# Preparing three heads at a time on 120 rows, with the first two inverses ordered on VectorE, in a chunked recurrence followed by an MLP

## The chip, the cores and the metric

The kernel runs on one core of a Trainium2 chip. The metric is the device time of one execution in microseconds (us); the median of several runs is compared. TensorE does the matmuls, VectorE and ScalarE the elementwise work and the copies out of PSUM, GpSimd (POOL) issues part of the DMAs, and SyncE (SP) issues the rest.

## The reference

For 4 batches and 8 heads a state of 40 x 40 is carried over 768 steps; its output goes through an MLP with the Mish function (`h * tanh(softplus(h))`):

```python
for t in range(S):
    y[:, :, t] = np.einsum('bhd,bhde->bhe', rt, state)
    Sa = np.einsum('bhde,bhe->bhd', state, at)
    state_decay = state * wt[:, :, None, :] - np.einsum('bhd,bhe->bhde', Sa, bt)
    state = state_decay + np.einsum('bhd,bhe->bhde', vt, kt)
...
h = x @ w_in                       # 3072 x 320 by 320 x 2048
sp = np.where(h > 20.0, h, np.log1p(np.exp(np.minimum(h, 20.0))))
g = h * np.tanh(sp)
return (g @ w_out).astype(np.float32)
```

## The kernel before, in words

The 768 steps are cut into 12 chunks of 64, and the chunks are worked in six pairs. Within a chunk the steps depend on each other through a triangular system, which is solved with an explicit inverse, so that all that is left to do in sequence is one pass for each chunk.

For each chunk there is a **preparation**, `pre_a`, called twice (`be` = 0, 1). A call holds two blocks of 40 rows (one for each dimension of a head), on partitions 0 to 39 and 64 to 103, with eight heads of the batches side by side: 80 of 128 partitions carry data. It loads `w` and `a` (L131, tile `wa`) and `b` and `k` (L134, tile `bk`) on SP's queue. VectorE forms the running products of `w` forward and backward with two scans (L147 and L157), after a small reduction (L145), reciprocals (L146, L156) and a copy (L150), and multiplies them into `a` (L152) and into `b` and `k` (L170). ScalarE copies `a` into the layout `ad` (L155). TensorE multiplies `ad` by `bk` (L186, 16 matmuls in the profile for each call, since a float32 matmul shows as two) and transposes `bk` (L202); four matmuls with the identity (L166) bring the chunk's decay factors into the tile `rw`. GpSimd writes the forward products to the DRAM scratch `pD`.

For each pair there is an **inverse**: `pre_inv` on VectorE alone, a transpose (L209), 30 elimination steps of two instructions each (L214 and L216, each step reading what the one before wrote), and two transposes (L218, L220). Then `post_inv` on TensorE and ScalarE (L232, L241, L258).

For each chunk there is a **step**, `step(c)`, which carries the state (L284, L293, L304, L314, L334 and L339 on TensorE; masks and state updates on VectorE, L316, L325, L342, L346). It writes its result to the DRAM scratch `yD`.

The **MLP** runs after the attention. Its float32 matmuls are done as sums of products of a high and a low part, so the weights are split first: w_in in 12 pieces and w_out in 8. The weights arrive as 64-bit floats: a piece is loaded as 512 KB (L453, tile `cv_d`), scaled on ScalarE (L459), put together in three VectorE instructions (L461 to L463), and split by ScalarE (L494) and VectorE (L495). Three of the w_in pieces (`early`, with `NQ0 = 1` quarter) are split at the beginning, beside the first pair; the other nine by `first`, when the last pair's preparation is over, with one buffer for each stage (`CVA = 1`). The w_out pieces follow. The x tiles are loaded from `yD` and `pD` and split on VectorE (L567, L569, L570). L585 is the first matmul of the MLP, L605 to L607 the second.

What sets the order: the program is written with a Tile scheduler that orders each engine's instructions by the order of the code and by priorities, the table `OFF` (a larger number moves an instruction's place further forward). Each engine then runs its list strictly in order. `ORDER = '0aiA1'` says what is written around a pair: step of the first chunk, preparation of a later pair (`a`), the next inverse (`i`), the weights (`A`), step of the second chunk. The letters of `QS` choose the queues of the loads (SP), and of the steps' loads, `yD` and `pD` (GpSimd).

## Time and profile before

| | us |
|---|---|
| median of 3 runs (lowest, highest) | 846.35 (843.54, 848.62) |
| the profiled execution | 842.54 |
| its span | 840.7 |
| beginning of inverse 0, end of inverse 0 | 48.7, 99.0 |
| beginning of inverse 5, end of inverse 5 | 383.5, 433.6 |
| first matmul of the MLP | 471.7 |

The profile is of one execution, and its times are counted from the start of its span. PE is TensorE's matmul, PEld its weight load, DVE is VectorE, ACT ScalarE, POOL GpSimd, SP SyncE. A row of a group names a line of the kernel, the engine, the operation, output<-input, how often it occurred, and then busy us, the mean of one in ns, and the idle time of the engine just before, with what ended it. PEclk is the share of the full clock that TensorE was granted. What bounds a stage is read from that stage's own window and from the waits in it, not from the mean over the span.

### The profile page before, as it was taken

Reading aid. Unit: us, or ns where it says so; the run is one execution under the profiler, and the core shown is the slowest. Engines: PE = TensorE matmul, PEld = TensorE weight load, DVE = VectorE, ACT = ScalarE, POOL = GpSimd, SP = SyncE. Lnnn points to the kernel's source line nnn. Section 1 sums busy time; section 2 is a strip of 40 time slices with the busy share of each in tenths; the row PEclk is TensorE's granted clock in tenths of the full one; section 3 lists DMA queues with packets and bytes.
Section 4 is the critical chain, followed back from the end, with each engine's and each line's share of the span. In section 5 each row is a group of like instructions: output and inputs, shape, how many; then the busy total and the mean of one; then the engine's idle time right before and its main releaser. Section 6 shows DMA issues by size and latency. Waiting matters only on the chain.

```text
span 840.7 us, 18817 instructions
## 1 busy us (share of the span) xinstructions
PE 737.5 (88%) x7816; PEld 688.5 (82%) x7816; DVE 463.3 (55%) x975; ACT 427.9 (51%) x937; POOL 103.3 (12%) x182
## 2 busy tenths in 40 slices
PE   2545898998989889888749999999999999999998
PEld 2444687887778778777648899999999999999998
DVE  6789889659879758947962649221222222122110
ACT  4533657774665766676457646333333333333331
POOL 8100021132123023211210200000000000000000
PEclk9755699899999999999978999999999999999999
DMA  6422232333333133313543744211120121100000
GB/s 173 139 72 64 82 78 67 96 75 94 89 96 88 57 86 98 96 26 98 139 123 82 186 132 127 54 39 32 38 54 29 26 54 36 35 20 16 16 1 32
DMA packets 58213, 61.92 MB, mean 74 GB/s; under 512 B 25536, under 2 KB 48704, under 8 KB 58128
## 3 DMA queue, kind: packets, MB, share of 16 engines
q1 hardware_dynamic: 49296, 40.94, 17.4%
q0 software_dynamic: 8832, 19.79, 9.4%
q8 instruction: 61, 1.00, 0.5%
q14 instruction: 24, 0.20, 0.1%
HBM read 48.79 MB, written 11.86 MB: 72 GB/s over the span
## 4 chain that ended last, share of the span: by engine, by line
PE 61%; ACT 15%; DVE 15%; DMA 5%; issue 4%; SPq 0%; POOL 0%; ACTq 0%; DVEq 0%
PE ph L585 20%; PE po L605 7%; PE po L606 7%; PE po L607 6%; PE pa L186 4%; PE pa L258 3%; PE pq L314 3%; PE pq L334 2%; DMA cv_d<-in_wi 2%; DVE XL L216 2%; DVE tmp L214 2%; ACT KT L260 2%; ACT bdT L250 1%; ACT bdT L249 1%; ACT ad L155 1%
## 5 line engine op out<-in xcount | busy, mean ns | idle before, releaser
L585 PE MATMUL ph<-xh,w_ih 128*128 128x256 f32 x576 | 148.9, 283 | 0.0
L587 ACT ACTIVATE g<-ph 128x512 f32<-128x512 f32 x96 | 57.3, 598 | 179.7 <-PE ph L585 179.7
L591 DVE TENSOR_TENSOR gl<-g,gh 128x1024 fp32r<-128x1024 f32 x48 | 58.6, 1224 | 160.3 <-ACT gh L590 160.0
L585 PE MATMUL ph<-xh,w_il 128*128 128x256 f32 x576 | 123.7, 283 | 0.0
L186 PE MATMUL pa<-bk,ad 128*128 128x168 f32 x384 | 85.5, 372 | 42.2 <-DVE bk L170 15.0
L606 PE MATMUL po<-w_ol,gh 128*128 128x320 f32 x384 | 118.6, 309 | 0.0
L607 PE MATMUL po<-w_oh,gl 128*128 128x320 f32 x384 | 118.3, 309 | 0.0
L605 PE MATMUL po<-w_oh,gh 128*128 128x320 f32 x384 | 117.8, 309 | 0.1
L585 PEld LDWEIGHTS ph<-xh,w_ih 128*128 128x128 f32 x576 | 109.5, 190 | 0.2 <-issue 0.2
L186 PEld LDWEIGHTS pa<-bk,ad 128*128 128x128 f32 x384 | 70.4, 232 | 47.6 <-issue 23.1
L585 PE MATMUL ph<-xl,w_ih 128*128 128x256 f32 x384 | 100.7, 284 | 0.0
L585 PEld LDWEIGHTS ph<-xh,w_il 128*128 128x128 f32 x576 | 96.2, 190 | 0.1
L585 PEld LDWEIGHTS ph<-xl,w_ih 128*128 128x128 f32 x384 | 73.1, 190 | 0.2 <-issue 0.2
L605 PEld LDWEIGHTS po<-w_oh,gh 128*128 128x128 f32 x384 | 71.8, 188 | 0.6 <-ACT w_oh L494 0.5
L606 PEld LDWEIGHTS po<-w_ol,gh 128*128 128x128 f32 x384 | 72.1, 188 | 0.2 <-DVE w_ol L495 0.2
L607 PEld LDWEIGHTS po<-w_oh,gl 128*128 128x128 f32 x384 | 72.1, 188 | 0.0
L216 DVE TENSOR_TENSOR XL<-XL,tmp 128x30 f32<-128x30 f32 (+9 forms) x180 | 58.8, 326 | 2.6
L214 DVE TENSOR_TENSOR tmp<-XL 128x30 f32<-128x30 f32 (+9 forms) x180 | 58.2, 323 | 2.6
L314 PE MATMUL pq<-bdr,UVT 128*128 128x128 f32 x384 | 55.2, 288 | 4.6 <-DVE UVQ L316 3.8
L258 PE MATMUL pa<-bdT,HA 128*104 128x128 f32 x384 | 52.7, 289 | 7.1 <-ACT bdT L251 4.8
L258 PEld LDWEIGHTS pa<-bdT,HA 128*104 128x104 f32 x384 | 47.2, 181 | 10.3 <-ACT bdT L251 5.9
L314 PEld LDWEIGHTS pq<-bdr,UVT 128*128 128x128 f32 x384 | 48.6, 197 | 7.0 <-DVE UVQ L316 4.9
(89 smaller groups left out, 1237.3 us busy)
## 6 DMA issues: line engine op xcount, KB each, us to landing
wa<-in_wa SPq DMA_DIRECT2D x48, 162.5 KB
bk<-in_bk SPq DMA_DIRECT2D x48, 160.0 KB
cv_d<-in_wi SPq DMA_DIRECT2D x12, 512.0 KB
cv_d<-in_wo SPq DMA_DIRECT2D x8, 640.0 KB
pD<-P POOLq DMA_DIRECT2D x48, 81.2 KB, 2.4
VS<-in_vN POOLq DMA_DIRECT2D x24, 160.0 KB, 3.3
UVT<-in_vD POOLq DMA_DIRECT2D x24, 160.0 KB, 4.0
bdr<-in_rD POOLq DMA_DIRECT2D x24, 160.0 KB, 4.5
```

Source lines behind the costliest of these rows:

```text
L186: PE.matmul(pt[:, j], ad[:, s0 + j].rearrange("p k a t -> p (k a t)"), bk[:, s0 + j], start=(j == 0), stop=True, skip_group_check=True)
L214: V.tensor_tensor(out=tv, in0=X[:, i + 1:32, i:i + 1].broadcast_to([128, 31 - i, i]), in1=X[:, i:i + 1, 0:i].broadcast_to([128, 31 - i, i] ...
L216: V.tensor_tensor(out=X[:, i + 1:32, 0:i], in0=X[:, i + 1:32, 0:i], in1=tv, op=ALU.add)
L258: PE.matmul(pk[:, j], ha[:, s0 + j], bd[:, s0 + j].rearrange("p a t -> p (a t)"), start=(j == 0), stop=True, skip_group_check=True)
L260: A.copy(kt[:, s0:s0 + 4], pk)
L314: PE.matmul(pq[:, s], UVT[:, g * 4 + s, be * 128:be * 128 + 128], br[:, be, g * 4 + s].rearrange("p a t -> p (a t)"), start=(s == 0), stop ...
L585: PE.matmul(o, w, x, start=(j == 0 and n == 0), stop=(n == 7), skip_group_check=True)
L587: A.activation(g[:, f0:f0 + 2], ph, AF.Mish)
L591: V.tensor_tensor(out=gl, in0=g, in1=gh.bitcast(F32), op=ALU.subtract)
L605: PE.matmul(po[k], gh[:, j, t], oh, start=(f == 0), stop=False, skip_group_check=True)
L606: PE.matmul(po[k], gh[:, j, t], ol, start=False, stop=False, skip_group_check=True)
L607: PE.matmul(po[k], gl[:, j, t], oh, start=False, stop=(f == 15), skip_group_check=True)
```

## The change

Four things change together.

First, the preparation is done once for each chunk and not twice. The new `pre_d(c)` holds the four blocks of 40 rows densely: three of them whole on 120 partitions, with eight slots each, and the fourth block's eight slots cut 3/3/2 and put beside them as slots 8 to 10. So each VectorE instruction of the preparation is over 120 rows and 11 slots. Then 12 DMAs for each chunk, on SP's queue (the new fifth letter of `QS`), bring the products within SBUF to where the matmuls want them, six for `a` (L179) and six for `b` and `k` (L185). The decay factors are gathered with six matmuls with columns of a new constant `sel` (the constants grow to 520 columns), and `pD` is written in six pieces for each chunk. The loads of a chunk are three whole tiles, `wz`, `ax` and `bx`, issued with a priority of their own (`'L': 300`); `pre_a` begins with the copy of `a` on ScalarE.

Second, no weights are split at the beginning: `NQ0 = 0`, so all 12 pieces of w_in come through `first`, with two buffers for each stage (`CVA = 2`).

Third, VectorE's beginning is ordered: the second pair's preparation is written with `issue_after` the last instruction of inverse 0 and gets the priority `'F': 600`; `ORDER0 = '0i1a'` replaces `ORDER` for the first pair; and the priority `'I1'` of inverse 1 goes from -15 to 400.

Fourth, the fills of the work tiles at the beginning move from VectorE to GpSimd and ScalarE.

```diff
-QS = "SGGG"
+QS = "SGGGS"
...
+ORDER0 = '0i1a'
...
-    def pre_a(c, be):
-        n = 2 * c + be
-        wa, bk, ad = wab[n % NWA], bkb[n % NWA], adb[n % 2]
-        for al in range(2):
-            q = slice(al * 64, al * 64 + 40)
-            LQ.dma_start(out=wa[q], in_=I['wa'][c, be, al])
-        for al in range(2):
-            q = slice(al * 64, al * 64 + 40)
-            LQ.dma_start(out=bk[q, :, 0:128], in_=I['bk'][c, be, al])
...
+    def parts():
+
+        for g in range(3):
+            yield g // 2, g % 2, slice(g * 40, g * 40 + 40), 0, 0, 8
+        for i in range(3):
+            yield 1, 1, slice(i * 40, i * 40 + 40), 8, 3 * i, min(3, 8 - 3 * i)
+
+    def pre_d(c):
+        wz = pw.tile([120, 716], F32, name="wz", bufs=NWZ)
+        a = pw.tile([120, 704], F32, name="ax", bufs=NAX)
+        bk = pw.tile([120, 11, 2, 64], F32, name="bx", bufs=NBX)
+        with at(tc, 'L'):
+            LQ.dma_start(out=wz, in_=I['wd'][c])
+            LQ.dma_start(out=a, in_=I['ad'][c])
+            LQ.dma_start(out=bk.rearrange("p s x t -> p (s x t)"), in_=I['bkd'][c])
...
+        V.tensor_tensor_scan(out=P, data0=wz[:, 0:715], data1=d1[:, 64:779], initial=0.0, op0=ALU.mult, op1=ALU.add)
...
+        V.tensor_tensor(out=a3, in0=a3, in1=P3[:, :, 0:64], op=ALU.mult)
+        for be, al, q, h, s, m in parts():
+            DQ.dma_start(out=ab[be][al * 64:al * 64 + 40, s * 64:(s + m) * 64], in_=a[q, h * 64:(h + m) * 64])
+        V.reciprocal(d1[:, 64:779:65], w2[:, 1])
+        V.tensor_tensor_scan(out=E[:, 0:714][:, ::-1], data0=wz[:, 2:716][:, ::-1], data1=d1[:, 1:715][:, ::-1],
+                             initial=0.0, op0=ALU.mult, op1=ALU.add)
+        V.tensor_tensor(out=bk, in0=bk, in1=E3[:, :, 0:64].unsqueeze(2).broadcast_to([120, 11, 2, 64]), op=ALU.mult)
+        for be, al, q, h, s, m in parts():
+            DQ.dma_start(out=bkb[be][al * 64:al * 64 + 40, s:s + m, 0:128], in_=bk[q, h:h + m].rearrange("p s x t -> p s (x t)"))
...
+    def pre_a(c, be):
+        if be == 0:
+            pre_d(c)
+        a, bk, ad = ab[be], bkb[be], adb[be]
...
     pa(0)
-    inv(0)
+
+    end = inv(0)
     for u in range(4):
-        with at(tc, 'P%d%d' % (u // 2, u % 2)):
+        with at(tc, 'F'), tc.issue_after(end):
             pre_a(2 + u // 2, u % 2)
...
-        for k in ORDER:
+        for k in ORDER if n else ORDER0:
...
-NQ0 = 1
+NQ0 = 0
...
-CVA = 1
+CVA = 2
```

The lines of the changed kernel stand about 30 further down: L209, L214, L216, L218 and L220 of the inverse become L239, L244, L246, L248 and L250; L186 becomes L216; L461 to L463 and L495 become L492 to L494 and L526; L567 becomes L598.

How the instructions move is seen at three places. In the rows below a number behind a tile's name tells buffers apart. The first is VectorE's list at the beginning. Before, where inverse 0 opens (L209), the second pair's preparation (L146, L147, L150, L152) stands between its instructions:

```order
L495 SCALAR_TENSOR_TENSOR w_il_928<-cv_w,w_ih_927 128x512
L191 TENSOR_TENSOR HA<-pa,cst 128x3x64
L191 TENSOR_TENSOR HA<-pa,cst 128x2x64
L193 TENSOR_TENSOR GP<-GP,cst 128x8x32
L146 RECIPROCAL d_102<-w_689 128x8
L209 STREAM_TRANSPOSE XL<-GP 128x32x32
L147 SCALAR_TENSOR_TENSOR P<-wa_96,d_102 128x520
L210 MEMSET XL 128x32
L214 TENSOR_TENSOR tmp<-XL 128x30
L150 COPY w_689<-P 128x8
L152 TENSOR_TENSOR wa_96<-wa_96,P 128x512
```

Now, on VectorE where inverse 0 closes (L250), its last steps stand alone and the second pair's preparation (L170 to L172) follows:

```order
L244 TENSOR_TENSOR tmp<-XL 128x58
L246 TENSOR_TENSOR XL<-XL,tmp 128x2x29
L244 TENSOR_TENSOR tmp<-XL 128x30
L246 TENSOR_TENSOR XL<-XL,tmp 128x30
L248 STREAM_TRANSPOSE TT<-XL 128x32x32
L250 STREAM_TRANSPOSE GP<-TT 64x32x32
L170 TENSOR_REDUCE w_696<-wz 120x11
L170 TENSOR_REDUCE w_823<-wz 120x11
L171 RECIPROCAL d_96<-w_696 120x11
L172 SCALAR_TENSOR_TENSOR P<-wz,d_96 120x715
```

So the preparation has moved from between the inverse's steps to behind all of them.

The second place is SP's queue at the beginning. Before, only the constants, a weight piece (`cv_d`) and the loads of the first two calls stand there:

```order
L136 DMA cst<-in_cst 128x328
L453 DMA cv_d<-in_wi 128x1024
L131 DMA wa_96<-in_wa 40x1040 x2
L134 DMA bk_98<-in_bk 40x8x128 x2
L131 DMA wa_97<-in_wa 40x1040 x2
L134 DMA bk_99<-in_bk 40x8x128 x2
```

Now, from row 5 of SP's list on, the loads of the next chunks stand between the transfers of the first one (`a` and `bk` here are the tiles that TensorE's side reads); the second `wz` below is row 11, and the row of `a_91` behind it is row 12:

```order
L160 DMA ax<-in_ad 120x704
L159 DMA wz<-in_wd 120x716
L161 DMA bx<-in_bkd 120x1408
L163 DMA cst<-in_cst 128x520
L179 DMA a_90<-ax 40x512 x2
L159 DMA wz<-in_wd 120x716
L179 DMA a_91<-ax 40x512
L179 DMA a_91<-ax 40x192 x2
L179 DMA a_91<-ax 40x128
L185 DMA bk_92<-bx 40x8x128 x2
```

A load of a later chunk that has to wait for its buffer thus stands ahead of transfers of an earlier chunk.

The third place is VectorE's list in inverse 5. Before, the split of one weight piece (L461, L462, L463, L495) is spread over four steps of the inverse:

```order
L461 TENSOR_SCALAR cv_w<-cv_m 128x512
L214 TENSOR_TENSOR tmp<-XL 128x168
L462 SCALAR_TENSOR_TENSOR cv_w<-cv_m,cv_w 128x512
L216 TENSOR_TENSOR XL<-XL,tmp 128x24x7
L463 SCALAR_TENSOR_TENSOR cv_w<-cv_d,cv_w 128x512
L214 TENSOR_TENSOR tmp<-XL 128x184
L216 TENSOR_TENSOR XL<-XL,tmp 128x23x8
L214 TENSOR_TENSOR tmp<-XL 128x198
L216 TENSOR_TENSOR XL<-XL,tmp 128x22x9
L495 SCALAR_TENSOR_TENSOR w_il_5065<-cv_w,w_ih_5064 128x512
```

Now, on VectorE in the same inverse, pieces follow each other within two or three steps, and the next piece's first instruction (L492) stands ahead of the last (L526) of the one before:

```order
L244 TENSOR_TENSOR tmp<-XL 128x184
L493 SCALAR_TENSOR_TENSOR cv_w<-cv_m,cv_w 128x512
L246 TENSOR_TENSOR XL<-XL,tmp 128x23x8
L494 SCALAR_TENSOR_TENSOR cv_w<-cv_d,cv_w 128x512
L244 TENSOR_TENSOR tmp<-XL 128x198
L246 TENSOR_TENSOR XL<-XL,tmp 128x22x9
L492 TENSOR_SCALAR cv_w<-cv_m 128x512
L526 SCALAR_TENSOR_TENSOR w_il_5150<-cv_w,w_ih_5149 128x512
L493 SCALAR_TENSOR_TENSOR cv_w<-cv_m,cv_w 128x512
L244 TENSOR_TENSOR tmp<-XL 128x210
L494 SCALAR_TENSOR_TENSOR cv_w<-cv_d,cv_w 128x512
L246 TENSOR_TENSOR XL<-XL,tmp 128x21x10
```

Between the first and the last transpose of inverse 5 stand ten whole splits, the last instructions of two more, and the products of the first x tile (L598, L600, L601), where before stood six whole splits.

107 lines of the change are left out of this document (56 added, 51 removed).

## The prediction

> **What bounds the kernel now.** I read the page's busy times first, then the timeline of VectorE to find where each inverse begins and ends, and then the stretches between those points.
>
> ```profile
> PE 737.5 (88%) x7816; PEld 688.5 (82%) x7816; DVE 463.3 (55%) x975; ACT 427.9 (51%) x937; POOL 103.3 (12%) x182
> ```
>
> TensorE is busy for 88% of the span, VectorE for 55%. That mean hides stages with different limits. In VectorE's timeline (start, duration, instruction) the transpose of L209 opens an inverse, and that of L220 closes it. These are the first and the last of the six inverses:
>
> ```profile
> 48.73 2.10 DVE L209 STREAM_TRANSPOSE XL<-GP 128x1024 f32<-128x1024 f32 x1
> 97.88 1.24 DVE L220 STREAM_TRANSPOSE GP<-TT 64x1024 f32<-64x1024 f32 x1
> 383.50 2.14 DVE L209 STREAM_TRANSPOSE XL<-GP 128x1024 f32<-128x1024 f32 x1
> 432.44 1.24 DVE L220 STREAM_TRANSPOSE GP<-TT 64x1024 f32<-64x1024 f32 x1
> ```
>
> The windows cut there, and once more at the first matmul of the MLP (471.7), give the stages; the columns are the length, and the busy time and count of PE, PEld, DVE, ACT and POOL, then PE's granted clock, DMA share and GB/s:
>
> ```profile
> 0.00:48.70 48.70, 23.04 (x111) 19.57 (x112) 34.40 (x67) 25.46 (x65) 19.55 (x36) 0.86 0.53 145
> 48.70:99.00 50.30, 27.35 (x170) 22.64 (x170) 46.88 (x117) 20.19 (x59) 5.08 (x10) 0.62 0.24 70
> 99.00:383.50 284.50, 255.35 (x3612) 223.34 (x3606) 216.39 (x536) 190.59 (x499) 58.20 (x105) 0.96 0.30 79
> 383.50:433.60 50.10, 34.63 (x556) 30.75 (x556) 45.66 (x116) 26.12 (x57) 13.96 (x21) 0.96 0.51 141
> 433.60:471.70 38.10, 31.90 (x536) 29.65 (x531) 15.47 (x27) 25.59 (x55) 2.73 (x4) 0.83 0.35 99
> 471.70:840.70 369.00, 365.21 (x2857) 362.58 (x2854) 104.46 (x117) 139.94 (x205) 3.76 (x6) 1.00 0.18 49
> ```
>
> In the first and the last inverse VectorE is the bound (46.88 of 50.30, 45.66 of 50.10); between them and after them TensorE is (255.35 of 284.50, or 0.898; then 365.21 of 369.00). TensorE takes its work in order, and the work after the last inverse stands behind it in both kernels, so the end is the moment at which the last inverse closes, plus what is left: 840.7 - 433.6 = 407.1 us. Four places decide: when inverse 0 closes, how much TensorE work then remains before inverse 5 can open, how long inverse 5 takes, and the tail.
>
> **Head: the first pair and inverse 0.** These are the preparation's VectorE groups (count | busy us, mean ns of one | idle before), now run 24 times:
>
> ```profile
> L145 DVE TENSOR_REDUCE w<-wa 128x8 f32<-128x256 f32 x24 | 9.8, 409 | 1.9 <-DMA wa<-in_wa 1.4 <-PE pa L166 0.4
> L146 DVE RECIPROCAL d<-w 128x8 f32<-128x8 f32 x24 | 4.8, 199 | 0.2
> L147 DVE TENSOR_TENSOR_SCAN P<-wa,d 128x520 f32<-128x520 f32 x24 | 29.6, 1235 | 0.3
> L152 DVE TENSOR_TENSOR wa<-wa,P 128x512 f32<-128x512 f32 x24 | 16.4, 682 | 0.0
> L157 DVE TENSOR_TENSOR_SCAN wa<-wa,d 128x519 f32<-128x519 f32 x24 | 29.6, 1233 | 6.8 <-ACT ad L155 6.7
> L170 DVE TENSOR_TENSOR bk<-bk,wa 128x1024 f32<-128x1024 f32 x24 | 29.1, 1212 | 1.4 <-DMA bk<-in_bk 1.3
> ```
>
> A dense chunk does each once, on rows longer by 11/8. Taking the time as proportional to the row: scans 2.468 x 1.375 = 3.39, products (1.212 + 0.682) x 1.375 = 2.60, reduce 0.56, and the two reciprocals and the small copy, whose length hardly depends on the row, 0.2 each: 7.15 us. Before, a chunk paid for the same eight instructions twice 5.37 us, 10.7. So 3.6 us of VectorE go per chunk, 43 us in twelve. Nearly all of that lies under TensorE's bound, so most of it can't show.
>
> The first pair gains less than its VectorE time. Products now wait for two transfers within SBUF behind VectorE; the nearest row is a DMA of similar size:
>
> ```profile
> pD<-P POOLq DMA_DIRECT2D x48, 81.2 KB, 2.4
> 14.96 4.84 PE L186 MATMUL pa<-bk,ad 128*128 128x168 f32 x16 [14.96 <-DVE bk L170]
> ```
>
> The first product started at 14.96. Afterwards SP's queue holds the third load of wz (row 11 of SP's order) ahead of the rest of the `a` transfers and all `bk` transfers, and that load waits until VectorE has read its buffer. The first load of wz heads SP's queue; with 2.4 us for it and somewhat less for the start, VectorE begins at about 4, and chunk 1's second scan ends 7.15 and another 5.5 later, near 16.6; the transfers then issue until about 20 and land 2.4 us later: first product near 22.4. Four half chunks follow, each a group of 16 matmuls with its transposes: one at the first one's 4.84 plus some 2, three at about 5.2. Inverse 0 opens near 45 (40 to 50). This estimate is the softest of the head; before, it opened at 48.73.
>
> Inverse 0 then runs with nothing between its steps:
>
> ```profile
> L216 DVE TENSOR_TENSOR XL<-XL,tmp 128x30 f32<-128x30 f32 (+9 forms) x180 | 58.8, 326 | 2.6
> L214 DVE TENSOR_TENSOR tmp<-XL 128x30 f32<-128x30 f32 (+9 forms) x180 | 58.2, 323 | 2.6
> L218 DVE STREAM_TRANSPOSE TT<-XL 128x1024 f32<-128x1024 f32 x6 | 11.7, 1944 | 0.1
> ```
>
> (58.8 + 58.2)/6 = 19.5, transposes 2.10 + 1.94 + 1.24 = 5.3, idle 5.2/6 = 0.9: 25.7 us. It closes near 71 instead of 99: **-28.0 us** (-33 to -23).
>
> **Middle: the second pair's TensorE work comes later.** It had run under inverse 0; `issue_after` now holds its VectorE work until the inverse closes, so TensorE idles for 26 us and pays this work afterwards. Its price is that of a pair in the stretch 99 to 383.5, where four pairs were prepared (length, PE busy; L186, L202, L166):
>
> ```profile
> 99.00:383.50 284.50, 49.03 (x256) 0.96 0.30 79
> 99.00:383.50 284.50, 21.68 (x126) 0.96 0.30 79
> 99.00:383.50 284.50, 3.35 (x64) 0.96 0.30 79
> ```
>
> (49.03 + 21.68 + 3.35)/4 = 18.5 us, and at 0.898 density 20.6: **+20.6** (18.5 to 26). After the idle TensorE starts slow: sixteen products took 4.84 us at 14.96, against 49.03/16 = 3.06 in this stretch; 1.8 for one half chunk, 3.6 for two: **+3.0** (1.3 to 5). The Trainium skill, "TensorE: Matmul & The Clock Gate", section "What's actually happening", says that an idle window of about 3.4 us halves the clock and that about 3.4 us of sustained work restores it; by that rule the loss would be about 1.7 us and the sum 1.3 us lower. The granted clock of 0.62 between 48.7 and 99 agrees with a half clock after idle stretches, but 4.84 us for one half chunk, all slow, is longer than that rule's window, so the row's value stays.
>
> What VectorE's 43 us are worth here is read from what TensorE waited for in this stretch (total us, times, longest):
>
> ```profile
> PE pu L293 <- ACT UVT L286: 5.8, 4, 3.2
> PE pa L202 <- ACT bkn L203: 5.6, 6, 1.2
> ...
> PE pa L232 <- DVE TT L218: 2.1, 4, 0.7
> ...
> PE pa L202 <- DVE HA L191: 1.5, 5, 0.5
> ...
> PE pq L334 <- DVE UVQ L316: 0.9, 2, 0.6
> PE pq L314 <- DVE UVQ L316: 0.9, 1, 0.9
> ```
>
> VectorE's lines are 5.4 us of some 29 idle; ScalarE's copies, which the change leaves, hold most. I take half of them: **-3.0** (-10 to 0). The transfers within SBUF replace loads on the same queue. One late load stood on the chain for 4.68 us:
>
> ```profile
> 210.62 4.68 DMA bk<-in_bk
> 391.75 4.62 DMA cv_d<-in_wi
> ```
>
> A transfer of 2.4 us issued a chunk ahead is no worse, so zero here, with the other answer as a rival. Inverse 5 opens near 71 + (255.35 + 18.5)/0.898 + 0 = 376 (before 383.5).
>
> **Inverse 5: the weights move into it.** `NQ0 = 0` sends three more pieces of w_in through `first`. Before, six whole splits stood between the transposes of inverse 5 and three followed; now ten, the last instructions of two more, and the first x tile's products. Mean times:
>
> ```profile
> L461 DVE TENSOR_SCALAR cv_w<-cv_m 128x512 int32<-128x512 int32 x12 | 5.5, 459 | 14.2 <-ACT cv_m L459 14.1
> L462 DVE SCALAR_TENSOR_TENSOR cv_w<-cv_m,cv_w 128x512 int32<-128x512 int32 x12 | 8.2, 686 | 0.2
> L567 DVE TENSOR_TENSOR xy<-xy,xp 128x768 f32<-128x768 f32 x12 | 11.5, 956 | 21.8 <-DMA xy<-yD 21.2 <-DMA xp<-pD 0.6
> L569 DVE TENSOR_TENSOR xl<-xy,xh 128x512 fp32r<-128x512 f32 x12 | 8.3, 692 | 60.6 <-ACT xh L568 60.6
> ```
>
> A split is 0.46 + 3 x 0.686 = 2.52 (L463 and L495 are as long as L462). Four more are 10.1, two last instructions 1.4, the x products about 2.1: 13.5 of VectorE time. VectorE idled 50.10 - 45.66 = 4.4 us there, and the load of 4.62 us in the fence before shows for what: with one buffer each load begins when the last piece is read. `CVA = 2` should take about 1.5 of that: **+12.0** (+9 to +26). TensorE can't use it: its order has no MLP matmul ahead of the post-inverse. The tail loses the three splits and the first x loads: **-2.0** (-5 to 0), since TensorE was busy 31.90 of 38.10 there.
>
> **The sum.** -28.0 + 20.6 + 3.0 - 3.0 + 12.0 - 2.0 = +2.6. The profiled execution was 842.54 us with a span of 840.7; the changed one would have a span of 843.3 and take 845.1. That execution lies 3.8 below the median of the runs, 846.35; on the median's level the forecast is **849 us**. About 0.5%, 4.2 us, is what a measurement of this kernel can tell from no change, so 842.1 to 850.6 counts as the same.
>
> **Rivals.**
>
> 1. *The head start is kept: faster.* VectorE's relief lifts TensorE's density in the stretch from 0.898 to 0.93, so 273.9 us of work take 294.5 instead of 305: -10 in place of -3. With inverse 5 at its lower end (+9) and the slow start at its own (1.3), the sum is -28 + 20.6 + 1.3 - 10 + 9 - 2 = -9.1: 837; with inverse 0 opening at 42, 834. For it: VectorE is full in both inverses shown, and a late inverse also delays ScalarE. Against: the waits above name ScalarE.
>
> 2. *SP's queue blocks: slower.* Twelve transfers a chunk stand in order with the loads. A load that waits for its buffer holds every transfer behind it, and each pair's first products with them. At 3 to 4 us, the order of the 4.68 us chain piece, for five pairs: +15 to +20, 864 to 869. It decides once the queue is late by more than the slack of a chunk. For it: rows 11 and 12 of SP's order are such a place. Against: this engine's queue has time after the first pair, with a DMA share of 0.30.
>
> 3. *Inverse 5 becomes bound by its loads: slower.* If they start 8.2 us after it opens, as before (391.75 against 383.50), and twelve run one after the other at 4.62, the last lands at 63.7; its split and the inverse's remaining steps make some 76: +26 instead of +12, 863. Against: two buffers, and the first pieces should be in before the inverse opens.
>
> That the change doesn't do what it says is possible only in the head: if the transfers hold inverse 0 until 50, the forecast becomes 854, inside the first case's own range.
>
> **How the numbers follow.** Forecast case 0.45, with its own range 842 to 858: 0.27 of it within 0.5%, 0.16 above, 0.02 below. Rival 1 has 0.30, all faster. Rival 2 has 0.15, slower. Rival 3 has 0.10, 0.09 slower and 0.01 the same. Faster 0.32, same 0.28, slower 0.40. The range must leave out no more than 0.2: 834 to 866 leaves out a third of rival 1 and half of rival 2, some 0.18.
>
> **What would show it.** Right: inverse 0 closes at 67 to 76; inverse 5 opens at 368 to 380 and takes 59 to 66 us; 403 to 407 us follow. Rival 1: density of 0.93 or more between them and an opening before 366. Rival 2: waits of TensorE's L216 (the products) for the transfers of `a` and `bk`, at every pair. Rival 3: VectorE's waits for ScalarE's `cv_m` during inverse 5 above 8 us. The forecast is wrong if inverse 5 stays near 50 us, or if inverse 0 doesn't close before 80.

## The result, and the profile after

The changed kernel takes 884.62 us (median of 4 runs, 883.08 to 888.0) against 844.94 for the kernel before in the same comparison (843.03 to 848.62): the ratio is 1.047, with a 95% interval of 1.0419 to 1.052. It is slower by about 40 us. The forecast was 849 with a range up to 866, so the time lies outside it.

The page's busy times come first, as for the kernel before:

```profile
PE 738.2 (84%) x7864; PEld 694.8 (79%) x7864; DVE 434.1 (49%) x877; ACT 427.7 (48%) x937; POOL 116.0 (13%) x208
```

VectorE has lost 463.3 - 434.1 = 29 us of work and TensorE has as much as before, yet the span grew from 840.7 to 882.3. So what was added is time in which TensorE is idle. These are the windows of the changed kernel, cut where inverse 0 opens (53.2) and closes (80.5), where inverse 1 opens (134.2), and where inverse 5 opens (408.0) and closes (474.8); the columns are those of the windows of before:

```profile
0.00:53.20 53.20, 20.06 (x116) 17.08 (x116) 19.74 (x35) 22.06 (x59) 22.00 (x42) 0.97 0.72 176
53.20:80.50 27.30, 1.86 (x50) 1.63 (x52) 25.13 (x66) 1.58 (x5) 0.00 (x0) 0.58 0.00 0
80.50:134.20 53.70, 44.10 (x555) 38.38 (x550) 36.22 (x64) 35.70 (x98) 17.90 (x34) 0.85 0.66 158
134.20:408.00 273.80, 242.36 (x3322) 215.24 (x3321) 184.40 (x453) 176.81 (x465) 55.60 (x102) 0.93 0.40 103
408.00:474.80 66.80, 33.86 (x471) 30.71 (x472) 59.30 (x139) 31.65 (x65) 13.96 (x20) 0.79 0.55 142
474.80:882.30 407.50, 395.90 (x3372) 391.78 (x3368) 109.30 (x125) 159.91 (x250) 6.51 (x10) 0.98 0.17 46
```

The order of the beginning is what the change asked for: inverse 0 stands alone (25.13 of 27.30 on VectorE, the DMA engines idle), and it closes at 80.5 instead of 99.1. But inverse 1, which opened 1.4 us after the first one closed, now opens 53.7 us after it. From inverse 1's opening to inverse 5's the kernel takes 273.8 us, where before it took 383.5 - 100.5 = 283.0. That part is shorter, but this doesn't show that it is faster: 555 matmuls stand in the stretch before it, and 3322 are left for it, where before 3612 stood between 99.0 and 383.5. Inverse 5 takes 66.8 instead of 50.1, and the tail is the same.

A window's length less PE's busy time is TensorE's idle time, which is a fairer measure here, since a window that holds more work doesn't count as a loss for that. Until inverse 0 opens it is 33.1 us (before 25.7), under inverse 0 25.4 (23.0), from there to inverse 5 41.0 (29.2), under inverse 5 32.9 (15.5), and after it 11.6 (10.0). The largest piece of the added idle time, 17.4 us, lies in inverse 5, the next, 11.8 us, between inverse 0 and inverse 5.

The first rows of TensorE in the changed kernel (start, duration, instruction, then the idle time before it and what ended it):

```profile
18.22 1.03 PE L190 MATMUL pa<-w,cst 120*64 120x16 f32 x12 [18.22 <-DMA cst<-in_cst]
29.03 4.68 PE L216 MATMUL pa<-bk,ad 128*128 128x168 f32 x16 [9.79 <-DMA bk<-bx]
42.97 4.18 PE L216 MATMUL pa<-bk,ad 128*128 128x168 f32 x16 [1.55 <-DMA bk<-bx]
```

The first product starts at 29.03, 14 us later than before, and what it waits for is a transfer within SBUF. Over the window up to inverse 0 the products wait twice for such a transfer (total us, times, longest):

```profile
PE pa L216 <- DMA bk<-bx: 11.3, 2, 9.8
```

Between the first two inverses these waits are 0.5 us in all, and from inverse 1 to inverse 5 the profile shows no wait of TensorE for a DMA. SP's queue ahead of the first product (start, time to issue, instruction):

```profile
17.64 0.34 SPq L159 DMA_DIRECT2D wz<-in_wd  x1
18.04 2.99 SPq L179 DMA_DIRECT2D a<-ax  x4
21.07 1.66 SPq L185 DMA_DIRECT2D bk<-bx  x2
23.28 0.34 SPq L160 DMA_DIRECT2D ax<-in_ad  x1
23.66 3.63 SPq L185 DMA_DIRECT2D bk<-bx  x4
```

One transfer takes SP about 0.75 (`a`) to 0.83 us (`b`, `k`) to issue. The chain of waits gives how long they then take to land, and the same for a load (start, length, what):

```profile
21.95 6.83 DMA bk<-bx
38.45 4.38 DMA bk<-bx
...
119.79 6.55 DMA wz<-in_wd
```

The two transfers of `b` and `k` took 6.83 and 4.38 us from the start of their issue, not 2.4, with the DMA engines at a share of 0.72 in that window. The last row is between the two first inverses: a load that had stood in SP's queue behind six transfers, as the next two rows show (SP's queue, then VectorE):

```profile
109.08 10.61 SPq L185 DMA_DIRECT2D bk<-bx  x6
119.79 0.47 SPq L159 DMA_DIRECT2D wz<-in_wd  x1
```

```profile
126.36 0.52 DVE L170 TENSOR_REDUCE w<-wz 120x11 f32<-120x352 f32 x1 [2.28 <-DMA wz<-in_wd]
```

The six transfers are issued only as TensorE leaves their tiles, which takes 10.61 us (between 100 and 125 SP's waits at L185 end with TensorE's matmuls: 4.5, 4.1 and 2.5 us); the load behind them lands at 126.3; VectorE, which takes its instructions in order, waits 2.28 us for it, and the products that TensorE needs from VectorE stand behind that.

### The profile page after: what moved, and what is told of

Its sections match the earlier page's. It is cut to its first block, busy times and chain, and to the rows that moved or that the text cites. A ratio compares the mean times of both kernels' runs of the same rounds, so it can differ in the third digit from the quotient of the medians.

```text
span 882.3 us, 18967 instructions
## 1 busy us (share of the span) xinstructions
PE 738.2 (84%) x7864; PEld 694.8 (79%) x7864; DVE 434.1 (49%) x877; ACT 427.7 (48%) x937; POOL 116.0 (13%) x208
## 4 chain that ended last, share of the span: by engine, by line
PE 60%; DVE 15%; ACT 13%; DMA 6%; issue 4%; SPq 2%; DVEq 0%; ACTq 0%
PE ph L616 20%; PE po L637 6%; PE po L638 6%; PE po L636 6%; PE pa L216 5%; PE pa L287 4%; PE pq L343 3%; DVE tmp L244 3%; DVE XL L246 3%; DMA bk<-bx 2%; PE pa L270 2%; PE pu L313 2%; PE pq L363 2%; PE pa L232 2%; ACT bdT L278 1%
## 5 line engine op out<-in xcount | busy, mean ns | idle before, releaser
L216 PE MATMUL pa<-bk,ad 128*128 128x168 f32 x384 | 78.6, 350 | 22.5 <-DMA bk<-bx 11.8
L216 PEld LDWEIGHTS pa<-bk,ad 128*128 128x128 f32 x384 | 64.4, 215 | 28.5 <-DVE HA L221 11.4
L287 PE MATMUL pa<-bdT,HA 128*104 128x128 f32 x384 | 60.6, 315 | 2.2 <-issue 0.9
L246 DVE TENSOR_TENSOR XL<-XL,tmp 128x30 f32<-128x30 f32 (+9 forms) x180 | 59.2, 329 | 4.2
L244 DVE TENSOR_TENSOR tmp<-XL 128x30 f32<-128x30 f32 (+9 forms) x180 | 58.8, 327 | 4.3
L261 PE MATMUL pa<-TT,GP 32*32 32x32 f32 x768 | 19.4, 200 | 49.7 <-DVE TT L248 47.6
L261 PEld LDWEIGHTS pa<-TT,GP 32*32 32x32 f32 x768 | 16.1, 114 | 54.5 <-DVE TT L248 48.9
L287 PEld LDWEIGHTS pa<-bdT,HA 128*104 128x104 f32 x384 | 55.2, 204 | 4.6 <-ACT bdT L280 1.7
```

The lines of the kernel that those rows point to most:

```text
L216: PE.matmul(pt[:, j], ad[:, s0 + j].rearrange("p k a t -> p (k a t)"), bk[:, s0 + j], start=(j == 0), stop=True, skip_group_check=True)
L244: V.tensor_tensor(out=tv, in0=X[:, i + 1:32, i:i + 1].broadcast_to([128, 31 - i, i]), in1=X[:, i:i + 1, 0:i].broadcast_to([128, 31 - i, i] ...
L246: V.tensor_tensor(out=X[:, i + 1:32, 0:i], in0=X[:, i + 1:32, 0:i], in1=tv, op=ALU.add)
L261: PE.matmul(px[al * 32:al * 32 + 32, j], gp[q, u, 0], TT[q, u], start=(j == 0), stop=True, skip_group_check=True)
L287: PE.matmul(pk[:, j], ha[:, s0 + j], bd[:, s0 + j].rearrange("p a t -> p (a t)"), start=(j == 0), stop=True, skip_group_check=True)
```

## The experiments

The theory after this reading (theory A) was a sum of three losses: the transfers in the first pair, about 8; the second pair's preparation taken out from under inverse 0, about 25; the weights in inverse 5, 17. The rival was that transfers and SP's queue delay every pair. Each run was compared with the kernel before on its own chip, whose median lay between 846 and 851; times are therefore compared by ratio (its 95% interval behind it), and stages by their lengths in one profiled execution. Where no number of executions is given, there were two.

**The order undone.** `e1_no_order` gives the changed kernel VectorE's old order.

```diff
-ORDER0 = '0i1a'
+ORDER0 = '0aiA1'
...
-       ... 'I1': 400, ...
+       ... 'I1': -15, ...
...
-        with at(tc, 'F'), tc.issue_after(end):
+        with at(tc, 'P%d%d' % (u // 2, u % 2)):
```

> The changed kernel with VectorE's beginning as before: no issue_after, the second pair's preparation under inverse 0 at its old priorities, ORDER for the first pair too, I1 at -15; dense preparation and late weights stay. Theory A (the loss is a sum of three: first pair's transfers +8, the second pair's preparation taken out from under inverse 0 about +25, weights in inverse 5 +17): inverse 0 opens near 53, lasts about 45, inverse 1 opens near 100 instead of 134, inverse 5 opens at 372 to 385 and still takes 65 to 68; 846 to 860 us. Rival B (the transfers within SBUF and SP's queue delay every pair, the order is harmless): inverse 5 opens at 400 or later, 875 us or more.

It took 887.98 us (ratio 1.0487, 1.0259 to 1.0714): nothing was won. Inverse 1 opens at 111.8, but then:

```profile
111.80:418.20 306.40, 270.21 (x3670) 238.84 (x3672) 188.75 (x465) 191.80 (x502) 61.19 (x110) 0.92 0.37 94
```

From there to inverse 5 it takes 306.4 us: what was won before inverse 1 was lost behind it. The middle term of theory A falls with this run; the rival's numbers (inverse 5 at 400 or later) came.

**The order alone, on the kernel before.** `e5_before_order` adds `ORDER0`, `'I1': 400`, `'F': 600` and `issue_after` to the kernel before.

```diff
+ORDER0 = '0i1a'
...
-    inv(0)
+    end = inv(0)
...
-        with at(tc, 'P%d%d' % (u // 2, u % 2)):
+        with at(tc, 'F'), tc.issue_after(end):
```

> The kernel before with the ordering alone: issue_after the end of inverse 0 with priority F for the second pair's preparation, ORDER0 for the first pair, I1 at 400. Theory A: inverse 0 closes near 75, inverse 1 opens near 130 to 140 instead of 100, inverse 5 opens 18 to 30 us later than 383.5; 860 to 873 us. Rival B: TensorE does the postponed work at its usual density and inverse 5 opens within 5 us of 383.5; 840 to 848 us.

847.55 us (8 runs; ratio 1.0012, 0.9959 to 1.0064): no difference that can be measured, as rival B had it. Its windows up to inverse 5:

```profile
0.00:50.00 50.00, 24.15 (x108) 21.26 (x108) 31.75 (x61) 23.72 (x62) 19.52 (x36) 0.90 0.54 141
50.00:79.00 29.00, 2.07 (x54) 1.68 (x54) 26.96 (x70) 3.34 (x7) 0.00 (x0) 0.58 0.04 11
79.00:118.30 39.30, 33.29 (x407) 29.41 (x402) 27.63 (x57) 29.75 (x83) 6.40 (x12) 0.87 0.31 87
118.30:387.50 269.20, 237.43 (x3326) 206.14 (x3323) 214.50 (x534) 179.56 (x472) 57.24 (x103) 0.97 0.32 83
```

This is how the prediction had the order: 20 us won when inverse 0 closes at 79, and given back by 387.5, because TensorE does the postponed work later. The same order on the dense preparation needs 53.7 us where this needs 39.3, between the first two inverses; of the 14.4 us, 44.10 - 33.29 = 10.8 are TensorE's work (555 matmuls against 407). From inverse 1 to inverse 5 the two kernels have nearly the same number of matmuls (3322 and 3326), and the changed one takes 273.8 - 269.2 = 4.6 us longer.

**The weights alone, on the kernel before.** `e4_before_late_weights`:

```diff
-NQ0 = 1
+NQ0 = 0
-CVA = 1
+CVA = 2
```

> The kernel before with NQ0 = 0 and CVA = 2 alone. Theory A: the three early pieces leave 7.5 us of VectorE time out of the stretch up to 99, so inverse 0 closes 3 to 7 us earlier, and inverse 5 takes 63 to 68 instead of 50.1: 849 to 856 us. Rival B: two buffers hide the loads and the pieces cost little, inverse 5 takes 50 to 55, 838 to 845 us.

860.74 us (two runs; ratio 1.0165, 0.9988 to 1.0343, which just includes no change; theory A had 849 to 856). The windows from inverse 0 to inverse 5's close:

```profile
50.90:102.30 51.40, 29.14 (x174) 24.90 (x176) 48.61 (x124) 21.59 (x62) 5.07 (x10) 0.63 0.33 98
102.30:382.20 279.90, 252.99 (x3684) 220.16 (x3680) 209.72 (x524) 190.18 (x497) 57.41 (x104) 0.97 0.30 76
382.20:450.50 68.30, 37.16 (x498) 33.50 (x493) 59.38 (x140) 32.38 (x67) 13.79 (x20) 0.79 0.53 140
```

Inverse 5 takes 68.3 us, as in the changed kernel. The expected 3 to 7 us at the beginning did not come: inverse 0 closes at 102.3. VectorE is no less busy under inverse 0 than before (48.61 us against 46.88), so other work has taken the place of the three splits.

**The transfers left out.** `e9_no_transfers` drops both groups of six.

```diff
-        for be, al, q, h, s, m in parts():
-            DQ.dma_start(out=ab[be]...
...
-        for be, al, q, h, s, m in parts():
-            DQ.dma_start(out=bkb[be]...
```

> The changed kernel without the 12 transfers within SBUF of each chunk (the tiles that TensorE reads keep their first fill, so the preparation's products never reach TensorE and the output is not the reference's); all else stays, the order of VectorE too. Theory A: the first product starts at about 20 instead of 29 and inverse 0 opens 8 to 10 us earlier, little else moves: 870 to 877 us. Rival B: SP's queue is what delays every pair, so the preparation of each pair comes earlier: below 860 us.

874.74 us (ratio 1.0331, 1.0148 to 1.0513), within theory A's numbers but for another reason: with the transfers gone, the load of the constants moved behind other loads in SP's queue, and the first matmul waited for it until 32.38. So the run was made again with the constants second in the queue:

```diff
             LQ.dma_start(out=wz, in_=I['wd'][c])
+            if c == 0:
+                LQ.dma_start(out=cst, in_=I['cst'])
...
         if c == 0:
-            LQ.dma_start(out=cst, in_=I['cst'])
```

> The changed kernel without the 12 transfers within SBUF of each chunk (TensorE reads first fills, so the output is not the reference's), and with the load of the constants second in SP's queue: without that, the run before it had its constants at 32 us and its first product at 33, which hid what the transfers cost. Theory A2 (apart from the weights, what the dense preparation loses is its transfers, by their own time and by what waits behind them; the order costs nothing): the first product starts at 12 to 18, inverse 0 opens at 38 to 45, inverse 5 at 378 to 386: 853 to 862 us, which is the time of the kernel before with late weights alone (860.7). Rival B2 (the dense preparation also loses elsewhere, by its sel matmuls, its larger loads or the pieces of pD): 868 us or more.

852.48 us (8 runs; ratio 1.0073, 1.0044 to 1.0103), just below what theory A2 had. Its windows up to inverse 5:

```profile
0.00:39.00 39.00, 21.16 (x116) 18.46 (x116) 20.02 (x36) 24.50 (x63) 22.08 (x42) 0.91 0.77 189
39.00:66.30 27.30, 1.92 (x52) 1.69 (x54) 25.13 (x66) 1.61 (x4) 0.00 (x0) 0.54 0.00 0
66.30:103.20 36.90, 30.08 (x342) 27.17 (x338) 31.70 (x53) 24.25 (x72) 12.18 (x24) 0.83 0.61 167
103.20:377.90 274.70, 250.66 (x3554) 219.61 (x3556) 187.10 (x468) 187.97 (x491) 64.30 (x116) 0.96 0.31 77
```

Against the changed kernel inverse 0 opens 53.2 - 39.0 = 14.2 us earlier, and the stretch to inverse 1 is 53.7 - 36.9 = 16.8 us shorter. From inverse 1 to inverse 5 the lengths are alike (274.7 and 273.8). So the changed kernel is 31.0 us behind when inverse 1 opens and 30.1 behind when inverse 5 opens. By TensorE's idle time the loss is spread more: 33.1 - 17.8 = 15.3 us before inverse 0 opens, 9.6 - 6.8 = 2.8 before inverse 1, and 31.4 - 24.0 = 7.4 from there to inverse 5. The two measures differ since this run has done 342 matmuls where the changed kernel has done 555, and does the others later. Either way about half of the loss falls before inverse 0 opens. Behind inverse 1 it reaches TensorE through VectorE; these are its two longest waits for VectorE there, in the changed kernel and then in this run:

```profile
PE pa L232 <- DVE HA L221: 5.6, 10, 1.2
PE pa L216 <- DVE HA L221: 5.1, 6, 3.3
```

```profile
PE pa L213 <- DVE HA L218: 3.0, 5, 1.4
PE pa L229 <- DVE HA L218: 1.7, 5, 0.6
```

All its waits for VectorE in that stretch are 16.0 us in the changed kernel and 6.9 here.

The run takes away more than the transfers. TensorE reads first fills, so it needn't wait for VectorE's product either, and it starts before it (TensorE, then VectorE):

```profile
10.89 4.19 PE L213 MATMUL pa<-bk,ad 128*128 128x168 f32 x16 [0.99 <-ACT ad L199]
```

```profile
11.41 1.63 DVE L182 TENSOR_TENSOR bx<-bx,E 120x1408 f32<-120x1408 f32 x1
```

That is worth about 2 us at the beginning: VectorE ends this product at 13.04, and it ends the second chunk's at 21.7, before TensorE starts on it at 24.23. The earlier constants are worth little against the changed kernel, whose first product waited for its transfer until 28.78, long after the constants (18.2). By its time the run is 8 us below the kernel before with late weights alone (860.74), on another chip. That suggests that the dense preparation would help if its moves were free; but some of these 8 us can be the waits that are missing.

**The transfers on other queues.** Two runs ask whether it is the place in SP's queue. `e6_transfers_on_gpsimd` sets `QS = "SGGGG"`:

> The changed kernel with the transfers on GpSimd's queue in place of SP's (QS = SGGGG). Theory Q (the loss is the order in SP's queue: transfers that wait for TensorE hold the loads behind them, and VectorE with its products waits for the loads): the stretch from inverse 0's end to inverse 1's opening shrinks from 53.7 to 36 to 44 and VectorE no longer waits for wz and bx; 865 to 875 us. Rival D (the loss is the transfers' own time and their share of the DMA engines): the stretch stays at 50 or more, 880 to 895 us, since GpSimd's queue also carries the steps' loads and pD.

907.02 us (ratio 1.0723, 1.0559 to 1.0887), worse than either theory allowed:

```profile
127.90:426.60 298.70, 241.37 (x3306) 214.22 (x3304) 186.72 (x454) 178.85 (x465) 116.65 (x206) 0.88 0.38 97
```

Inverse 0 opens at 45.2, 8 us earlier than in the changed kernel, the stretch between the first inverses stays at 55.4, and the middle loses 25, with GpSimd's busy time at 116.65 there instead of 55.60. The second moves only `b` and `k` of the first two pairs:

```diff
-            DQ.dma_start(out=bkb[be]...
+            (A if c < 4 else DQ).dma_start(out=bkb[be]...
```

> The changed kernel with the transfers of b and k of the first two pairs (chunks 0 to 3) issued by ScalarE; those of a, and everything later, stay on SP. Theory I (the first two pairs lose by the time that twelve transfers take to issue one after the other, about 0.75 us each, and by what waits between them in SP's queue): first product at 18 to 23 instead of 29, inverse 0 opens at 44 to 49, the stretch from inverse 0 to inverse 1 takes 40 to 48 instead of 53.7; 862 to 875 us. Rival D (the landing time under the load of the DMA engines): the first product at 26 or later, 879 us or more.

896.0 us (ratio 1.0566, 1.0473 to 1.0659). TensorE's first product and ScalarE around it:

```profile
27.94 3.70 PE L216 MATMUL pa<-bk,ad 128*128 128x168 f32 x12 [8.77 <-ACT ad L202]
```

```profile
21.01 5.45 ACTq L185 DMA_DIRECT2D bk<-bx  x3
26.50 0.18 ACT L192 COPY rw<-pa 128x32 f32<-128x32 f32 x1 [7.66 <-DMA bk<-bx]
26.59 1.90 ACT L202 COPY ad<-a 64x512 f32<-64x512 f32 x3
```

ScalarE's own copies, for which TensorE waits, now stand behind three transfers, which keep its queue for 5.45 us at 0.80 us each to issue. Theory I's numbers did not come. Rival D's did (first product at 26 or later, 879 us or more), but by this other cause. That doesn't show that issuing is cheap, only that each of the other queues has work of its own that is held up.

**The loads moved.** `e10_loads_unhurried` takes the loads' priority away (`'L': 0`):

> The changed kernel with the priority of the dense loads taken away (L at 0), so that in SP's queue the transfers of a chunk stand closer to their products and the constants come fourth. Theory Q: the first product comes at 23 to 26 instead of 29, inverse 0 opens at 47 to 50, but later loads stand behind transfers that wait for TensorE, so VectorE waits for more loads between the inverses; 878 to 890 us in all. Rival D (the loads that run ahead take the DMA engines from the transfers): the transfers land within 3 us, each pair gains, 865 to 875 us.

887.76 us (ratio 1.0495, 1.036 to 1.063). The first product comes at 24.90, as theory Q had it, but inverse 0 opens at 56.2 and not at 47 to 50, because the next group of products waits until 36.63, for nothing that the profile names. `e17_loads_behind` holds the second pair's loads behind chunk 1's last transfer:

```diff
-        with at(tc, 'L'):
+        with at(tc, 'L'), tc.issue_after(moved[1]) if c in (2, 3) else nullcontext():
```

> The changed kernel with the loads of the second pair (chunks 2 and 3) held behind chunk 1's last transfer in SP's queue (issue_after); they then have the time of inverse 0, in which the DMA engines are idle. Theory M (bytes: the loads that run ahead share the DMA engines with the transfers): the transfers land within 3 to 4 us, first product at 22 to 25 instead of 29, inverse 0 opens at 44 to 48; 870 to 879 us. Theory N (count: the issue and latency of twelve DMAs one behind the other): without the loads between them the transfers still take their 9 us to issue, first product at 26 or later, inverse 0 at 50 or later; 880 us or more.

881.81 us (two runs; ratio 1.0357, 1.0313 to 1.0402).

```profile
74.50:128.90 54.40, 44.22 (x555) 39.30 (x550) 35.87 (x62) 35.90 (x98) 17.92 (x34) 0.85 0.65 156
```

The first product comes at 20.73, earlier than either theory had it, and inverse 0 opens at 47.1, 6.1 us earlier, as theory M had it; the stretch between the inverses is no shorter, and the time is theory N's.

**The bytes taken away.** `e18_tiny_transfers` keeps twelve transfers a chunk and cuts each to 128 bytes a partition:

```diff
-...s * 64:(s + m) * 64], in_=a[q, h * 64:(h + m) * 64])
+...s * 64:s * 64 + 32], in_=a[q, h * 64:h * 64 + 32])
...
-...s:s + m, 0:128], in_=bk[q, h:h + m]...
+...s, 0:32], in_=bk[q, h, 0, 0:32])
```

> The changed kernel with all twelve transfers of each chunk, each cut to 32 numbers a partition (128 bytes; the rest of the products never reaches TensorE, so the output is not the reference's). Theory M: the time comes near that without transfers, 852 to 862 us, inverse 0 opens at 39 to 46, the stretch from inverse 0 to inverse 1 takes 37 to 44. Theory N: nearly nothing is gained, 876 to 885 us, with inverse 0 at 50 or later and that stretch at 50 or more.

874.13 us (two runs; ratio 1.0267, 1.0191 to 1.0343).

```profile
0.00:49.90 49.90, 21.23 (x116) 17.76 (x116) 19.05 (x36) 22.05 (x59) 21.93 (x42) 0.93 0.64 150
...
77.20:120.00 42.80, 36.73 (x437) 33.41 (x432) 33.56 (x54) 31.27 (x87) 13.48 (x26) 0.82 0.51 124
```

Both theories are half right, each in its own place: the stretch is theory M's, the beginning nearly theory N's, and the time lies between them. The first product and the transfer that it waits for (TensorE, then the chain):

```profile
22.92 4.84 PE L216 MATMUL pa<-bk,ad 128*128 128x168 f32 x16 [4.72 <-DMA bk<-bx]
```

```profile
19.97 2.70 DMA bk<-bx
```

The transfer lands in 2.70 us instead of 6.83, and the first product comes 6.1 us earlier; but inverse 0 opens only 53.2 - 49.9 = 3.3 us earlier, of the 14.2 by which it opens earlier without transfers. So fewer bytes alone don't win back the beginning. Between the first two inverses they are worth 53.7 - 42.8 = 10.9 of 16.8. Here the matmuls in the stretch are fewer too (437), so this length has the same weakness as above.

**The weights held back.** `e12_weights_held` puts the pieces' VectorE instructions behind the last one of inverse 5:

```diff
-                    inv(n + 1)
+                    end = inv(n + 1)
...
-                with at(tc, 'W'):
+                with at(tc, 'W'), tc.issue_after(end):
```

> The changed kernel with the twelve weight pieces' VectorE instructions held behind the last instruction of inverse 5 (issue_after in the last pair). Theory W (the splits between the inverse's steps are what lengthen inverse 5): it takes 33 to 42 us instead of 66.8; afterwards the splits are bound by their loads, 12 at 4.6 us, and stand ahead of the first x tile on VectorE, so the first matmul of the MLP comes 50 to 60 us after inverse 5 instead of 38: 862 to 873 us. Rival L (the loads, or TensorE's steps in that window, set its length): it stays at 55 us or more, and the time grows to 890 us or more.

869.19 us (two runs; ratio 1.0276, 1.009 to 1.0462), the time that theory W expected. Its stages went further than it had them, inverse 5 to 31.0 us (33 to 42 expected) and the way to the MLP to 64.7 (50 to 60). Inverse 5, and what lies between it and the MLP's first matmul:

```profile
410.20:441.20 31.00, 24.31 (x362) 21.94 (x363) 29.36 (x82) 15.39 (x35) 9.55 (x14) 0.94 0.28 76
...
441.20:505.90 64.70, 46.60 (x659) 41.07 (x657) 45.28 (x83) 43.32 (x88) 9.93 (x14) 0.79 0.57 161
```

Without splits inverse 5 takes 31.0 instead of 66.8; 24 of these 36 us are given back behind it (872.5 - 441.2 = 431.3 us from there to the end, instead of 407.5), since the splits and the first x tile now come there. On the kernel before only the last six pieces were held, with `CVA = 2`:

> The kernel before with two buffers for the late weight pieces (CVA = 2) and the VectorE instructions of the last six pieces held behind the last instruction of inverse 5; the three early pieces stay early, three are split inside inverse 5. Theory W (a split within the inverse lengthens it by its own 2.5 us, and VectorE has time for it in the 38 us after): inverse 5 takes 38 to 44 us instead of 50.1 and the MLP begins 37 to 41 us after it; 833 to 841 us. Rival T (TensorE sets the end of that stretch, or the pieces come too late for the MLP): 843 us or more.

845.68 us (10 runs; ratio 0.9975, 0.9943 to 1.0007): the same, as rival T had it.

```profile
385.50:430.60 45.10, 37.70 (x566) 33.75 (x566) 38.59 (x100) 21.65 (x48) 11.11 (x17) 0.89 0.45 118
430.60:472.50 41.90, 32.96 (x524) 30.02 (x520) 23.50 (x44) 29.91 (x64) 6.31 (x9) 0.88 0.51 131
```

Inverse 5 is 5 us shorter and the way from it to the MLP 4 us longer. With six splits it makes no difference on which side of the inverse's end they stand; in the changed kernel, where ten stand in front of it, holding them back won some 15 us (869.19 against 884.62).

**Both repairs.** `e16_after_held_and_act` joins `e14`'s edit and the holding of the last six pieces, as in `e15`.

> The changed kernel with both repairs: the transfers of b and k of chunks 0 to 3 on ScalarE, and the last six weight pieces held behind inverse 5. If the losses add, it is the time with the transfers moved less 12 to 20 us: inverse 5 takes 46 to 54 us instead of 66.8, the MLP begins 38 to 44 us later; 846 to 862 us. If the two losses overlap, 863 us or more.

Two runs, 873.14 and 887.93 us, too far apart for a ratio, and the stages are not read. Both lie in the second case's range (863 or more), and neither is near the kernel before. But the ranges were set before `e14` turned out at 896: the lower run is 23 us below that, so whether the two losses add stays open.

**Dense from the third pair on.** `e19_dense_from_third_pair` prepares chunks 0 to 3 as the kernel before did, in its order, and chunks 4 to 11 densely; the loads have no priority, and the last six weight pieces are held behind inverse 5.

```diff
+ND = 4
...
+        if c < ND:
+            bk, ad = pre_o(c, be)
+        else:
+            if be == 0:
+                pre_d(c)
...
+                        if n == 2:
+                            x.enter_context(tc.issue_after(old['inv']))
+                            x.enter_context(tc.issue_after(old['load']))
```

> The first two pairs (chunks 0 to 3) prepared as in the kernel before, in its order and without transfers; from the third pair on the dense preparation with its transfers, the third pair's held behind inverse 0 and behind the earlier loads; no early weights, the last six pieces held behind inverse 5. If the transfers cost only where TensorE has nothing else to do: inverse 1 opens at 97 to 104, inverse 5 at 368 to 379 (before: 100.5 and 383.5), takes 44 to 50 us, 407 to 411 follow: 824 to 839 us, faster than both kernels. If they cost in every pair, as the prediction's second rival had it: inverse 5 opens at 383 or later, 842 us or more.

858.5 us (4 runs; ratio 1.0073, 1.0051 to 1.0095). The numbers are those of the prediction's second rival: 842 us or more, and inverse 5 opens at 403.9, not before 383. Inverse 1 opens early, at 95.2, but it takes 76.9 us instead of 48.8:

```profile
95.20:172.10 76.90, 62.21 (x777) 55.80 (x772) 60.88 (x137) 41.77 (x106) 23.90 (x46) 0.83 0.58 138
```

and in it VectorE waits for the loads and transfers of the dense preparation (total us, times, longest):

```profile
DVE w L182 <- DMA wz<-in_wd: 6.6, 1, 6.6
DVE bx L195 <- DMA bk<-bx: 4.2, 1, 4.2
```

So the loss is not tied to the first two pairs. The longest single stretch of it is where the dense preparation starts, and has no lead yet: inverse 1 is 28 us longer, and inverse 5 opens 403.9 - 383.5 = 20.4 us later. That the later pairs lose nothing is not shown by this run.

## Why the prediction was wrong, point by point

Against the prediction's own terms, by the two profiled executions (882.3 - 840.7 = 41.6 in all):

| term | forecast | measured |
|---|---|---|
| inverse 0 closes earlier | -28.0 | 80.5 - 99.0 = -18.5 |
| from there to inverse 5 | +20.6 | 327.5 - 284.5 = +43.0 |
| inverse 5 | +12.0 | 66.8 - 50.1 = +16.7 |
| after it | -2.0 | 407.5 - 407.1 = +0.4 |

One of the prediction's own signs of being wrong came: inverse 0 closed at 80.5, not before 80.

1. *The step that failed* is the price of the transfers within SBUF: "A transfer of 2.4 us issued a chunk ahead is no worse, so zero here", and in the head "the transfers then issue until about 20 and land 2.4 us later". Nothing in the trace of before showed such a transfer: the row taken for it was a write to DRAM of 81.2 KB, and a whole transfer of `b` and `k` has 160 KB. They landed in 6.83 and 4.38 us, and at 0.75 to 0.83 us to issue, twelve hold SP's queue for 9 to 10 us a chunk, which was counted in part for the head and not at all for the middle. The first product, forecast near 22.4, came at 29.03. Of these 6.6 us VectorE has 1.0 (SP's load in row 11, the fourth of `wz` and not the third, went out at 17.64 where 16.6 was forecast), the issue about 1, and the landing 4.4. Without the transfers inverse 0 opened 14.2 us earlier, and from its close to inverse 5's opening it took 311.6 us instead of 327.5. These 30 us are most of the 39.0 (41.6 against 2.6) by which the sum was short, and about 2 of them can be the other waits that this run took away; its span of 849.1 us is 5.8 above the 843.3 that the sum gave.

2. *Rival 2 was the right mechanism with the wrong size and place.* It named SP's queue and rows 11 and 12, and gave 3 to 4 us for each of five pairs. The queue did hold loads behind transfers that wait for TensorE. Over the whole run SP waited twelve times ahead of a transfer of `b` and `k` for the transposes that read the tile (total us, times, longest):

```profile
SPq L185 <- PE pa L232: 75.6, 12, 18.1
```

But the sign that the rival gave, waits of TensorE's products for the transfers at every pair, came only in the first pair (11.3 us) and hardly in the second (0.5). Against the run without transfers the distance was 14.2 us when inverse 0 opened, 31.0 at inverse 1 and 30.1 at inverse 5, so it did not grow from pair to pair. What later pairs lost shows in TensorE's waits for VectorE (16.0 us instead of 6.9).

3. *The order* was right. The head start is given back by TensorE's postponed work: in `e5` it takes 387.5 - 79.0 = 308.5 us from inverse 0's close to inverse 5's opening, 24.0 more than before, where the forecast had 20.6 + 3.0. The order alone made 1.0012. The slow start after the idle was not measured by itself; the granted clock in the stretch behind inverse 0 is 0.85 in the changed kernel and 0.87 in `e5`.

4. *VectorE's relief* was put at -3 us (bounds -10 to 0). TensorE's idle time from inverse 0's close to inverse 5's opening is 37.8 us with the same order on the old preparation (`e5`), 30.9 with the dense one without transfers (`e11`), and 41.0 in the changed kernel. So up to about 7 us of relief were there, and the transfers took more than that back.

5. *Inverse 5*, forecast at 62.1 us, took 66.8, within the bounds of +9 to +26. That is the late weights' doing: `e4` has it at 68.3 with the old preparation. VectorE's busy time in it rose by 59.30 - 45.66 = 13.6, which is the 13.5 of the prediction; the idle time didn't shrink as assumed, but grew from 4.4 to 7.5. Of that, 2.6 us are a wait for the first x tile and 2.4 us waits for ScalarE's `cv_m`, so rival 3's sign, 8 us or more of the latter, did not come.

6. *The tail* gained nothing, since TensorE sets its pace in both kernels.

Taken one after the other, the spans are: late weights 858.9 - 840.7 = +18.2; dense preparation without its transfers, with the order, against that, 849.1 - 858.9 = -9.8; the transfers 882.3 - 849.1 = +33.2. They add up because each is the difference to the one before; they are spans of single profiled executions, on different chips, and by `e4`'s ratio the late weights would be 14 us, with an interval that reaches zero. Three things stay open. How the 14 us at the beginning divide between issue time, landing time and the place of the loads is known only in part: the loads' place is worth 6.1, the bytes 3.3, and these two may overlap. More buffers for the tiles that the transfers write, so that they needn't wait for TensorE, were not tried. And a queue on which the transfers hold up nothing was not found.

## What to carry to other kernels

Where work is packed more densely and the result must then be moved, count the moves: each has an issue time on its queue, a landing time under the load of that moment, and a place in a queue where it can hold a load behind a tile that isn't free yet. In this kernel that cost showed most where the receiving engine had nothing else to do, at the beginning of the pipeline, while the saving on an engine that wasn't the bound showed hardly at all. And before a piece of preparatory work is moved to the end, see what bounds the stage it moves into: three splits whose early place had cost nothing that `e4` could show went into the last inverse, which became some 17 us longer.

## What the runs showed of the hardware

- A transfer within SBUF over 40 partitions took SP 0.75 us to issue even at 128 bytes a partition (four in 2.96 us), while a load of 336 KB took 0.34.
- Transfers of 160 KB landed in 6.83 and 4.38 us from the start of their issue where the DMA engines' share was 0.72; one cut to 5 KB landed in 2.70 us where it was 0.64 (`e18`). The Trainium skill, "DMA: Bandwidth & Descriptors", section "Anatomy of one DMA — SWDGE (gpsimd) path", gives about 2.0 us fixed and the bytes at 436 GB/s for that path, by which 160 KB would be an estimated 2.4 us. These were issued by SP, on busy DMA engines, and took 2.9 and 1.8 times that; the measurement decides.
- The Trainium skill, the same page, section "Issuing engines are not separate DMA queues", says that DMAs of all engines run on the same 16 DMA engines, and that issuing from several saves only the time to issue, "which is usually small relative to the DMA itself". No run here tests the sharing by itself: on GpSimd's queue the beginning was 8 us shorter and the whole longer. But the time to issue was not small here: twelve transfers hold a queue for 9 to 10 us, and on ScalarE three of them kept the queue for 5.45 us (`e14`), behind which its own copies stood.
